# Carrying the recurrent state every 64 tokens instead of every 128, with 64x64 products four at a time, in batches 2 to 4 of an mLSTM and Fourier-mixing kernel

## The chip, the core and the metric

The kernel runs on one core of a Trainium2 chip. Its engines work side by side, each through its own queue in order: TensorE (PE in the profile: matmuls; PEld: its loads of stationary operands), VectorE (DVE), ScalarE (ACT), GpSimd (POOL) and SyncE (SP, which here issues the transfers). PSUM is the memory that TensorE writes; it has eight banks of 128 partitions x 512 fp32 numbers. The metric is the device time of one execution in microseconds; lower is better.

## The reference

There are two parts, one after the other. The first is an mLSTM cell for 4 batches, 8 heads, 768 tokens and head dimension 40. Per head it carries a 40x40 state `C`, a vector `n` and a stabilizing maximum `m`:

```python
m_new = np.maximum(f_gate[:, :, t] + m, i_gate[:, :, t])
f_stab = np.exp(f_gate[:, :, t] + m - m_new)
i_stab = np.exp(i_gate[:, :, t] - m_new)
C = f_stab * C + i_stab * outer(vt, kt)
n = f_stab * n + i_stab * kt
y[:, :, t] = sigmoid(o) * (C @ qt) / max(|n . qt|, 1)
```

The second part takes `y` as a (4, 768, 320) array `x`, and computes `u = x + real(fft over tokens and features of x)`, a normalization over the 320 features, and `u + relu(un @ w_ch1) @ w_ch2` with 1280 hidden features.

## The kernel before

**Tiling.** A batch's 768 tokens are 6 chunks of 128 (`L`, `NT`). Within a chunk the recurrence is a masked product, as in attention; between chunks a state of 41 columns per head (`C` and `n` together) is carried. Heads are held in pairs: the first head of a pair lies on partitions 0 to 39, the second on 64 to 103 (`hip` is 0 or 1). Per chunk of batches 2 to 4 (`b` is 1 to 3) the steps are:

- `mlstm_exp` (L421): 8 exponentials on ACT make the weights `W` of 128 x 128 per head. `mlstm_mask` (L443, POOL) zeroes what lies in the future.
- `mlstm_scores` (L465): 8 matmuls, keys by queries, 40 rows x 128 columns. `mlstm_weigh` (L471, DVE) multiplies them by `W`.
- `mlstm_scale_q` (L431) and `mlstm_scale_v` (L437), both POOL, make the decayed queries `qg` and the weighted values `vw`.
- `mlstm_from_state` (L479): 4 matmuls of 128 x 128 by 128, the state's share of the output, into a PSUM tile `ph`. `mlstm_from_chunk` (L486): 8 matmuls with 41 output columns add the chunk's own share.
- `mlstm_to_state` (L496): 8 matmuls make the state's new part `pc`; `mlstm_decay` (L455, POOL) and `mlstm_gather` (L513 or L515, DVE) update the state.
- `mlstm_gather` also copies `ph` to `hT` in SBUF (L517 to L528, ACT). `mlstm_turn` (L540) transposes `hT` by 4 matmuls with the identity, to `px`. `mlstm_finish` (L549 to L555) is five DVE operations that divide, apply the output gate and write the chunk's `x`.

The second part follows per batch: folding and Fourier products (`mix_...`), and the MLP (`mlp_...`: L861 for the first batch's first layer, L986 for its second; L923, L928 and L1042 for the later batches).

**Order.** Nothing is reordered after the program is written. A plan of slots fixes the order: `at(slot, phase, fn)` puts a step into a slot, and `run` issues the steps by slot and phase, on every engine in this order. Each slot has one step of some batch's MLP at phase `MAIN` (2); the chunks' work of a later batch is filled around it, at `FILL` (1) for other engines and `FILL_PE` (3) for TensorE. Chunk `c` of batch `b` begins at slot `s = s0 + 3c`, with `s0` 0, 32, 50, 82. From slot s + 3 on comes a block of TensorE work: from-state of chunk c, scores of chunk c + 1, from-chunk and to-state of chunk c. The turned output follows up to five slots later.

**PSUM.** Four banks belong to the MLP and the mixing (`bank`). Two are a ring for scores (`ps_s`), two a ring for `ph`, `pc` and `px` (`ps_h`): a new tile takes the bank whose last tile has been read. The program's accesses by two engines to one bank of a tile are put in program order with semaphores, reads after reads too.

## Time and profile before

| | |
|---|---|
| Time, median of 3 runs | 416.13 us (415.49 to 417.23) |
| The profiled execution's span, first to last instruction | 414.0 us |
| So what lies around the span, against the median | 2.1 us |
| TensorE busy | 404.0 us, 98% |
| VectorE busy | 289.3 us, 70% |
| ScalarE busy | 188.8 us, 46% |
| GpSimd busy | 115.7 us, 28% |

The profile names each group of instructions by line, engine, operation and tile. A matmul of fp32 data shows as two records, so 8 matmuls are x16. A timeline row gives the start in us from the span's start, the time from the first start to the last end, and what was run. As matmuls are pipelined, rows overlap: the time that TensorE gives to a group is the distance to the next group's start. In square brackets stands how long the engine was idle ahead of a row, and for whom.

### The profile page before, as it was taken

How to read it: one execution, taken by the hardware profiler on the slowest of the kernel's cores; microseconds unless marked ns; L12 is line 12 of the kernel's file. 1: busy time of each engine (PE TensorE's matmuls, PEld its weight loads, DVE VectorE, ACT ScalarE, POOL GpSimd, SP SyncE). 2: the span in 40 equal slices, each digit the busy share in tenths (PEclk: the TensorE clock that was granted, in tenths of full speed). 3: DMA queues.
4: the chain of work that ended last, by engine and by line, in shares of the span. 5: the costliest groups of instructions: out<-in, count | busy, mean ns of one | idle time of the engine just before them, and what ended most of it. 6: DMA issues, size and time to landing. Idle time of an engine off the chain costs nothing.

```text
span 414.0 us, 8020 instructions
## 1 busy us (share of the span) xinstructions
PE 404.0 (98%) x2966; PEld 304.2 (73%) x2966; DVE 289.3 (70%) x682; ACT 188.8 (46%) x493; POOL 115.7 (28%) x194
## 2 busy tenths in 40 slices
PE   8999999999999999999999999999999999999997
PEld 6877555666667778776559998976559988555996
DVE  8789894978885548777874569787863786335652
ACT  6986366686651232655455413745551113355000
POOL 5554201567442420342061430342040000020000
PEclk9999999999999999999999999999999999999999
DMA  7899298479564154266100544310000000000010
GB/s 227 291 251 334 71 275 265 132 223 289 187 193 148 61 153 143 63 213 205 45 0 2 156 152 132 95 50 1 0 2 0 33 32 34 0 0 2 22 43 32
DMA packets 20549, 47.14 MB, mean 114 GB/s; under 512 B 2784, under 2 KB 9312, under 8 KB 20384
## 3 DMA queue, kind: packets, MB, share of 16 engines
q1 hardware_dynamic: 20512, 46.65, 36.6%
q8 instruction: 23, 0.38, 0.4%
q14 instruction: 14, 0.11, 0.1%
HBM read 42.52 MB, written 4.11 MB: 113 GB/s over the span
## 4 chain that ended last, share of the span: by engine, by line
PE 88%; DVE 8%; ACT 2%; POOL 1%; issue 1%; ACTq 0%; DVEq 0%
PE po L1042 18%; PE pm L923 17%; PE po L986 8%; PE pm L928 6%; PE ph L486 5%; PE pm L861 5%; PE ps L465 5%; PE ph L479 4%; PE pu L740 3%; PE px L540 2%; PE pm L852 2%; PE pz L709 2%; PE put L783 2%; PE pc L496 1%; PE pz L697 1%; DVE stats L767 1%
## 5 line engine op out<-in xcount | busy, mean ns | idle before, releaser
L992 DVE SCALAR_TENSOR_TENSOR x<-po,rstd,x 128x160 f32<-128x160 f32 (+1 forms) x69 | 27.0, 394 | 41.1 <-PE po L1042 35.5
L932 DVE TENSOR_TENSOR h<-h,pm 128x384 f32<-128x384 f32 x60 | 30.6, 550 | 30.4 <-PE pm L928 17.4
L421 ACT ACTIVATE W<-W,colT 128x128 f32<-128x128 f32 x144 | 45.1, 395 | 0.0
L443 POOL TENSOR_SCALAR_AFFINE_SELECT W<-W 128x1024 f32<-128x1024 f32 x18 | 22.4, 1247 | 75.4 <-ACT W L421 54.5
L923 PE MATMUL pm<-uT,w_sb 128*128 128x384 f32 x90 | 37.5, 504 | 0.2 <-DVE uT L911 0.2
L986 PE MATMUL po<-w_sb,h 128*128 128x320 f32 x120 | 34.4, 435 | 0.0
L471 DVE TENSOR_TENSOR W<-ps,W 128x512 f32<-128x512 f32 x48 | 30.7, 681 | 2.6 <-POOL W L443 2.3
L861 PE MATMUL pm<-uT,w_sb 128*128 128x384 f32 x80 | 29.7, 498 | 0.1
L986 PEld LDWEIGHTS po<-w_sb,h 128*128 128x128 f32 x120 | 22.3, 190 | 9.4 <-issue 0.8
L1042 PE MATMUL po<-T,S 128*128 128x160 f32 x180 | 27.9, 302 | 0.3 <-DVE x L992 0.3
L788 ACT COPY uT<-put 128x384 f32<-128x384 f32 x24 | 11.2, 478 | 37.1 <-PE put L783 37.1
L465 PE MATMUL ps<-qk 40*128 40x128 f32 x384 | 27.4, 282 | 0.0
L465 PEld LDWEIGHTS ps<-qk 40*128 40x128 f32 x384 | 23.9, 188 | 4.6 <-issue 0.7
L1042 PEld LDWEIGHTS po<-T,S 128*128 128x128 f32 x180 | 25.5, 190 | 1.7 <-DVE x L992 0.5
L1042 PE MATMUL po<-w_sb,h 128*128 128x160 f32 x180 | 26.5, 302 | 0.0
L524 ACT COPY h<-ph 41x512 f32<-41x512 f32 (+1 forms) x16 | 9.3, 582 | 37.1 <-PE ph L486 37.0
L1042 PEld LDWEIGHTS po<-w_sb,h 128*128 128x128 f32 x180 | 25.2, 190 | 1.3 <-DVE x L992 0.3
L431 POOL TENSOR_TENSOR qg<-qk,Gb 128x512 f32<-128x512 f32 x18 | 26.1, 1449 | 0.1
L486 PE MATMUL ph<-W,kvt 128*41 128x128 f32 x384 | 25.8, 277 | 0.0
L923 PEld LDWEIGHTS pm<-uT,w_sb 128*128 128x128 f32 x90 | 15.4, 190 | 13.2 <-DVE h L932 6.0
L479 PEld LDWEIGHTS ph<-qg,C 128*128 128x128 f32 x160 | 20.2, 192 | 5.5 <-POOL qg L431 1.6
L979 ACT ACTIVATE h<-h 128x384 f32<-128x384 f32 x45 | 23.1, 521 | 2.0 <-DVE h L932 2.0
(207 smaller groups left out, 844.5 us busy)
## 6 DMA issues: line engine op xcount, KB each, us to landing
W<-M_d SPq DMA_DIRECT2D x18, 512.0 KB
kvt<-in_kv SPq DMA_DIRECT2D x24, 324.0 KB
qk<-in_qkT SPq DMA_DIRECT2D x48, 160.0 KB
raw<-in_w SPq DMA_DIRECT2D x10, 640.0 KB
Gb<-G_d SPq DMA_DIRECT2D x36, 128.0 KB
so<-in_o SPq DMA_DIRECT2D x24, 160.0 KB
out<-x SPq DMA_DIRECT2D x24, 160.0 KB
ds_sb<-in_dft_s SPq DMA_DIRECT2D x1, 1155.0 KB
```

The lines of the kernel that those rows point to most:

```text
L421: nc.scalar.activation(out=k.W[:, h, :], in_=M, func=AF.Exp, scale=-1.0, bias=colT[:, c, 0, b * H + h:b * H + h + 1])
L431: nc.gpsimd.tensor_tensor(out=k.qg, in0=k.qk[:, 0], in1=k.Gb, op=OP.mult)
L465: nc.tensor.matmul(k.ps[hip][:, p, :], k.qk[r, 1, p, :], k.qk[r, 0, p, :], start=True, stop=True)
L471: nc.vector.tensor_tensor(out=Wv, in0=k.ps[hip], in1=Wv, op=OP.mult)
L479: nc.tensor.matmul(k.ph[:, p, :], k.C[:, p, :], k.qg[:, p, :], start=(p == 0), stop=False, skip_group_check=True)
L486: nc.tensor.matmul(k.ph[hip * 64:hip * 64 + D1, p, :], k.v1[:, 2 * p + hip, :], k.W[:, 2 * p + hip, :], start=(c == 0 and p == 0), stop=Tr ...
L861: nc.tensor.matmul(k.pm[i], w1_sb[:, ch, f0:f0 + L], u[2 * ch], start=(ch == 0 and not ahead), stop=(ch == 1 and ahead), skip_group_check= ...
L923: nc.tensor.matmul(bank, w, u, start=start, stop=True, skip_group_check=True)
L932: nc.vector.tensor_tensor(out=h, in0=h, in1=bank, op=OP.add)
L986: nc.tensor.matmul(k.po, hidden(gr, f)[:, i * L:(i + 1) * L], w2_sb[:, f, :], start=(f == 0), stop=(f == NFF - 1))
L992: nc.vector.scalar_tensor_tensor(out=u, in0=po, scalar=k.rstd[:, c:c + 1], in1=u, op0=OP.mult, op1=OP.add)
L1042: nc.tensor.matmul(po, a[:, f], w[:, f], start=start and f == 0, stop=f == half - 1, skip_group_check=True)
```

## The change

In batches 2 to 4 the recurrence inside a chunk is done in two halves of 64 tokens (`LH`), and the state is carried from half to half. The first batch keeps its form.

- Each of the four products becomes 16 matmuls on 64x64 tiles: 64 or fewer rows, 64 columns, 64 (or 41) moving columns, in the order `TILES`, so that four in a row use the four quarters of the array. Scores and to-state stand together ahead of the second part of from-chunk; from-chunk is split in two (`turn` 0 and 1), as the quarters change banks, with a small ACT copy (`halves_between`) between.
- `W` holds 64 columns per head: half the bytes are loaded (two transfers), exponentiated and weighed; the mask takes two POOL operations.
- The state is updated twice per chunk (`halves_decay`, `halves_add`), once for each half, in full-width operations instead of one per `hip`.
- Two PSUM tiles of two banks each, `scores` and `heads`, take the place of the rings. Scores use the first half of each bank, `pc` the second half of the same; `ph` uses the first half of the two heads banks and `px`, the turned output, the second half. `halves_order` is a small ACT copy that reads both.
- The turned outputs come at slots s0 + 8, 11, 14, 17, 20, 20; `mlstm_finish` follows in the next slot (for the fifth chunk, in the same one).
- Decays and weights for halves are made once, in the first batch's slots 8 to 18 (`halves_of_chunks`).
- The layouts of `q`, `k`, `v` and the spread table change on the host to match.

```diff
--- before.py
+++ after.py
...
-    ps_s = pool("ps_s", 2, space=PSUM)
-    ps_h = pool("ps_h", 2, space=PSUM)
+    ps_s = pool("ps_s", 1, space=PSUM)
+    ps_h = pool("ps_h", 1, space=PSUM)
...
+    scores = ps_s.tile([L, 2, NP * L], FP, name="ps")
+    heads = ps_h.tile([L, 2, NP * L], FP, name="ph")
+    whole = {id(t): iter(range(10**6)) for t in (scores, heads)}
+    def whole_bank(t, *shape):
+        part = t[:, next(whole[id(t)]) % 2, 0:int(np.prod(shape))]
+        return part.rearrange("p (a b) -> p a b", b=shape[-1]) if len(shape) > 1 else part
...
+    states = [t.rearrange("p n t -> p (n t)")[:, i * 2 * L:(i + 1) * 2 * L] for t in C_bufs for i in range(2)]
...
+        def halves_of_chunks(step):
+            half, end = M[0:BH, :, LH:], M[0:BH, :, LH - 1:LH].to_broadcast([BH, NT, LH])
+            if step == 0:
+                late["G"], late["K"] = (gp.tile([BH, NT, LH], FP, name=n) for n in ("G2", "K2"))
+                nc.gpsimd.tensor_tensor(out=late["G"], in0=end, in1=half, op=OP.subtract)
+                nc.gpsimd.tensor_tensor(out=late["K"], in0=a[:, :, 0:LH], in1=end, op=OP.subtract)
+            elif step == 1:
+                nc.scalar.activation(out=g[0:BH, :, LH:], in_=late["G"], func=AF.Exp)
+                nc.scalar.activation(out=wk[:, :, 0:LH], in_=late["K"], func=AF.Exp)
+            elif step == 2:
+                d2 = late["dec2"] = w2_sb[0:BH, 0, 0:BH // 2 * NS].rearrange("p (n c) -> p n c", c=NS)
+                ends = g[0:BH].rearrange("p c (i t) -> p (c i) t", i=2)[:, :, LH - 1]
+                nc.gpsimd.tensor_tensor(out=d2, in0=ends.unsqueeze(1).to_broadcast([BH, BH // 2, NS]),
+                                        in1=spread_sb[:, L:].unsqueeze(2).to_broadcast([BH, BH // 2, NS]), op=OP.mult)
+            elif step == 3:
+                p2 = bank("p2", [L, NT * BH + BH // 2 * NS], 2)
+                pt, pd = p2[:, 0:NT * BH], p2[:, NT * BH:]
+                late["p2"] = [t.rearrange("p (n c) -> p n c", c=n) for t, n in ((pt, BH), (pd, NS))]
+                for c in range(NT):
+                    nc.tensor.transpose(late["p2"][0][:, c, :], wk[:, c, :], ident[0:BH, 0:BH])
+                nc.tensor.matmul(late["p2"][1], spread_sb[:, 0:L], late["dec2"], start=True, stop=True)
+            else:
+                pt, pd = late["p2"]
+                nc.vector.tensor_copy(out=colT[:, :, 1, H:], in_=pt[:, :, H:])
+                nc.vector.tensor_copy(out=decB[:, NP:], in_=pd[:, NP:])
...
+        for n, (s, phase) in enumerate(((8, FILL + 0.55), (10, FILL + 0.75), (12, FILL + 0.5), (17, FILL_PE + 0.5),
+                                        (18, FILL + 0.75))):
+            at(s, phase, halves_of_chunks, n)
...
     def mlstm_load_max(b, c):
         k = chunks[b, c]
-        k.W = wp.tile([L, H, L], FP, name="W", tag="W")
-        nc.sync.dma_start(out=k.W, in_=M_d[c, b * H:(b + 1) * H, :].unsqueeze(0).to_broadcast([L, H, L]))
+        k.W = wp.tile([L, H, L], FP, name="W", tag="W").rearrange("p h t -> p (h t)")[:, 0:H * LH]
+        k.W = k.W.rearrange("p (h t) -> p h t", t=LH)
+        for i in range(2):
+            nc.sync.dma_start(out=k.W[i * LH:(i + 1) * LH],
+                              in_=M_d[c, i, b * H:(b + 1) * H, :].unsqueeze(0).to_broadcast([LH, H, LH]))
...
     def mlstm_mask(b, c):
-        W = chunks[b, c].W
-        nc.gpsimd.affine_select(out=W, in_=W, compare_op=OP.is_ge, fill=0.0, base=0, pattern=[[0, H], [1, L]],
-                                channel_multiplier=-1)
+        for i in range(2):
+            W = chunks[b, c].W[i * LH:(i + 1) * LH]
+            nc.gpsimd.affine_select(out=W, in_=W, compare_op=OP.is_ge, fill=0.0, base=0, pattern=[[0, H], [1, LH]],
+                                    channel_multiplier=-1)
+    def product(out, w, x, start):
+        nc.tensor.matmul(out, w, x, start=start, stop=True, skip_group_check=True)
...
+    sides = heads.rearrange("p hip (s m t) -> p s hip m t", s=2, t=L)
+    TILES = ((0, 0), (1, 1), (0, 1), (1, 0))
+    def wide(t, n):
+        return t[:, n:n + LH]
+    def halves_scores(b, c):
+        k = chunks[b, c]
+        n = NP * LH
+        k.ps = scores[:, :, 0:n].rearrange("p hip (m t) -> p hip m t", t=LH)
+        k.pc = scores[:, :, n:n + NP * D1].rearrange("p i (m d) -> p i m d", d=D1)
+        for p in range(NP):
+            for hip, i in TILES:
+                r, t = slice(hip * 64, hip * 64 + D), slice(i * LH, (i + 1) * LH)
+                product(k.ps[t, hip, p, :], k.qk[r, 1, p, t], k.qk[r, 0, p, t], True)
+    def halves_to_state(b, c):
+        k = chunks[b, c]
+        for p in range(NP):
+            for i, hip in TILES:
+                if 2 * c + i < NS - 1:
+                    r, h = slice(i * LH, (i + 1) * LH), hip * NP + p
+                    product(k.pc[hip * 64:(hip + 1) * 64, i, p, :], wide(k.k[r], h * D), k.vw[r, h, :], True)
+    def halves_state(k, i):
+        return k.C[i][:, 0:NP * D1].rearrange("p (m d) -> p m d", d=D1)
+    def halves_decay(b, c, i):
+        k, n = chunks[b, c], 2 * c + i
+        if 0 < n < NS - 1:
+            nc.gpsimd.tensor_tensor(out=halves_state(k, i + 1), in0=halves_state(k, i),
+                                    in1=decB[:, b * NP:(b + 1) * NP, n].unsqueeze(2).to_broadcast([L, NP, D1]), op=OP.mult)
+    def halves_add(b, c, i):
+        k, n = chunks[b, c], 2 * c + i
+        if n == 0:
+            nc.vector.tensor_copy(out=halves_state(k, 1), in_=k.pc[:, 0])
+        elif n < NS - 1:
+            nc.vector.tensor_tensor(out=halves_state(k, i + 1), in0=halves_state(k, i + 1), in1=k.pc[:, i], op=OP.add)
+    def halves_weigh(b, c):
+        k = chunks[b, c]
+        W = k.W.rearrange("p (hip m) t -> p hip m t", hip=2)
+        nc.vector.tensor_tensor(out=W, in0=k.ps, in1=W, op=OP.mult)
+    def halves_from_state(b, c):
+        k = chunks[b, c]
+        k.ph = sides[:, 0]
+        for m in range(2):
+            for i in range(2):
+                for hip, side in TILES:
+                    if 2 * c + i > 0:
+                        r, t, p = slice(hip * 64, hip * 64 + D), slice(i * LH, (i + 1) * LH), 2 * m + side
+                        product(k.ph[side * 64:(side + 1) * 64, hip, m, t], wide(k.C[i][r], p * D1), k.qg[r, p, t],
+                                m == 0 and i == (c == 0))
+    def halves_from_chunk(b, c, turn):
+        k = chunks[b, c]
+        for m in range(2):
+            for i, side in TILES:
+                hip = i ^ turn
+                r, h = slice(i * LH, (i + 1) * LH), hip * NP + 2 * m + side
+                product(k.ph[side * 64:(side + 1) * 64, hip, m, r], wide(k.v[r], h * D1), k.W[r, h, :], False)
+    def halves_between(b, c):
+        nc.scalar.copy(out=warm[0:1, 0:1], in_=chunks[b, c].ph[0:1, 1, 1, L - 1:L])
+    def halves_order():
+        nc.scalar.copy(out=warm[0:1].rearrange("p (a b) -> p a b", b=2), in_=heads[0:1, :, 0:NP * L:2 * L])
+    def halves_gather(b, c):
+        k = chunks[b, c]
+        k.hT = hT_bufs[(b * NT + c) % 2]
+        mlstm_heads(b, c, k.ph)
+    def halves_turn(b, c):
+        k = chunks[b, c]
+        px = sides[:, 0 if c == NT - 2 else 1]
+        for p in range(NP):
+            nc.tensor.transpose(px[:, p // 2, p % 2], k.hT[:, p, :], ident)
+        k.px = px
...
-        h1 = k.px.rearrange("p pr (two e) -> p (pr two) e", two=2)
+        px = k.px.rearrange("p (a pr) t -> p a pr t", a=2) if b == 0 else k.px
+        h1 = px.rearrange("p a pr (two e) -> p a (pr two) e", two=2)
...
+    def plan_halves(b, s0, stride=3):
+        for c in range(NT):
+            s = s0 + stride * c
+            end = c == NT - 1
+            t = 22 + 2 * c if b == 1 and c < 3 else s - 5
+            at(t, FILL, mlstm_load, b, c)
+            at(t, FILL, mlstm_load_max, b, c)
+            at(t, FILL, mlstm_load_decay, b, c)
+            at(s, FILL, mlstm_load_o, b, c)
+            at(s - 1, FILL, mlstm_scale_v, b, c)
+            at(s, FILL, mlstm_exp, b, c, 0)
+            at(s, FILL_PE + 2.05, halves_scores, b, c)
+            at(s, FILL_PE + 2.5, halves_to_state, b, c)
+            for i in range(2):
+                at(s + i, FILL + 0.05, halves_decay, b, c, i)
+                at(s + 1 + i, FILL - 0.2, halves_add, b, c, i)
+            at(s + 1, FILL - 0.5, mlstm_exp, b, c, NP)
+            at(s + 1, FILL, mlstm_mask, b, c)
+            at(s + 1, FILL + 0.1, mlstm_scale_q, b, c)
+            at(s + 2, FILL, halves_weigh, b, c)
+            at(s + 3, MAIN - 0.1 if end else FILL_PE, halves_from_state, b, c)
+            at(s + 3, MAIN - 0.1 if end else FILL_PE, halves_from_chunk, b, c, 0)
+            at(s + 3, MAIN if end else FILL_PE + 0.5, halves_between, b, c)
+            at(s + 3, FILL_PE + 3, halves_from_chunk, b, c, 1)
+            at(s + 4, FILL, halves_gather, b, c)
+            at(s + 4, FILL + 0.35, mlstm_tanh, b, c)
+            t = s0 + (8, 11, 14, 17, 20, 20)[c]
+            if c < NT - 2:
+                at(t - 1, FILL + 0.3, halves_order)
+            at(t, FILL_PE + 0.5 if c < NT - 2 else MAIN - 0.1, halves_turn, b, c)
+            if c < NT - 1:
+                at(t + 1, FILL + 0.05, halves_order)
+            first = c == NT - 2
+            at(t + (not first), MAIN + 0.55 if first else FILL + 0.05, mlstm_finish, b, c)
...
-        plan_mlstm(b, s_mlstm)
-        done = [s_mlstm + 3 * (j + NT // 2) + 7 + (b > 0 and j == 0) for j in range(NT // 2)]
+        (plan_halves if b > 0 else plan_mlstm)(b, s_mlstm)
+        done = [s_mlstm + n for n in ((16, 19, 22) if b == 0 else (18, 21, 22))]
```

## The prediction

> **What bounds the kernel now.** I read first the page's busy shares, then TensorE's groups by shape, then the timeline around a chunk's block, and last TensorE's waits.
>
> ```profile
> PE 404.0 (98%) x2966; PEld 304.2 (73%) x2966; DVE 289.3 (70%) x682; ACT 188.8 (46%) x493; POOL 115.7 (28%) x194
> ...
> PE   8999999999999999999999999999999999999997
> ...
> DVE  8789894978885548777874569787863786335652
> ```
>
> TensorE is the bound in every slice; DVE is near it in many (8 and 9 tenths). So TensorE time taken out counts in full, until a wait takes its place.
>
> ```profile
> L465 PE MATMUL ps<-qk 40*128 40x128 f32 x384 | 27.4, 282 | 0.0
> ...
> L486 PE MATMUL ph<-W,kvt 128*41 128x128 f32 x384 | 25.8, 277 | 0.0
> ...
> L479 PE MATMUL ph<-qg,C 128*128 128x128 f32 x160 | 21.5, 278 | 2.0 <-POOL qg L431 1.0 <-ACT C L511 0.8 <-DVE x L555 0.2
> ...
> L496 PE MATMUL pc<-vw,kvt 128*40 128x41 f32 x320 | 9.5, 202 | 0.0
> ```
>
> These are the four products. The next view is the timeline of the third batch-2 block (ordered by start):
>
> ```profile
> 105.29 1.29 DVE L471 TENSOR_TENSOR W<-ps,W 128x512 f32<-128x512 f32 x2
> ...
> 106.49 0.15 DVE L549 TENSOR_SCALAR den<-px 128x8 f32<-128x8 f32 x1
> ...
> 106.99 2.44 ACT L421 ACTIVATE W<-W,colT 128x128 f32<-128x128 f32 x8
> ...
> 107.65 0.49 DVE L555 TENSOR_TENSOR x<-px,so 128x320 f32<-128x320 f32 x1
> ...
> 108.21 1.05 PE L479 MATMUL ph<-qg,C 128*128 128x128 f32 x8
> ...
> 109.19 1.16 PE L465 MATMUL ps<-qk 40*128 40x128 f32 x16
> ...
> 110.28 1.07 PE L486 MATMUL ph<-W,kvt 128*41 128x128 f32 x16
> ...
> 111.19 0.48 PE L496 MATMUL pc<-vw,kvt 128*40 128x41 f32 x16
> ...
> 111.59 0.91 PE L861 MATMUL pm<-uT,w_sb 128*128 128x384 f32 x2
> ```
>
> The block takes 111.59 - 108.21 = 3.38 us. A turn's 4 records take 0.44 us (112.34 to 112.78), so a record of 128 columns takes 110 ns. From-state is 8 of these, 0.88; the other products' 16 records run two at a time: 0.88, 0.88, and 8 x 110 x 41/128 = 0.28 for to-state. What is left, 0.46, is the cost of changing the tile shape, 0.1 to 0.2 each time. `mlstm_finish` takes 1.65 us (106.49 to 108.14) and here ends 0.07 us ahead of from-state. Earlier in this batch:
>
> ```profile
> 96.99 0.60 PE L540 MATMUL px<-ident,h 128*128 128x128 f32 x4
> ...
> 97.63 0.17 DVE L549 TENSOR_SCALAR den<-px 128x8 f32<-128x8 f32 x1 [0.35 <-PE px L540]
> ...
> 98.08 1.05 PE L479 MATMUL ph<-qg,C 128*128 128x128 f32 x8
> ...
> 98.82 0.49 DVE L555 TENSOR_TENSOR x<-px,so 128x320 f32<-128x320 f32 x1
> ```
>
> Here from-state starts 1.23 us ahead of the end of finish: today the two use different banks.
>
> **What the Trainium skill says.** "TensorEngine Tiling (Array Packing)", Tiling Modes: 64x64 gives four independent tiles, and a change of mode drains the array; the 0.1 to 0.2 us agree with the second, no run here shows four tiles. "TensorE: Matmul & The Clock Gate", Wait — 56ns, not 53.3ns?: starts never come closer than about 25 ns. The trace differs: to-state's 16 records, each 202 ns, fit into 0.48, so their starts are (480 - 202)/15 = 19 ns apart. "PSUM — Partial Sum Buffer", PSUM bank collisions raise a hardware error: two engines mustn't touch one bank and quadrant at once, even at other columns. So a turned output that DVE still reads blocks TensorE's next write into that bank.
>
> **The change, part by part.**
>
> *Products.* Each of the four becomes 16 matmuls, 32 records of 64 columns, in 8 rounds of four. A round takes 110/2 = 55, say 57 ns; to-state too, as its loads are now 64 wide. Bounds: 57 ns if four overlap, 105 if only two do or starts keep 25 ns apart. I take 57, since pairs overlap fully in both directions today. Rounds per batch: scores 48, from-chunk 48, from-state 44, to-state 44: 184 x 0.057 = 10.5 us, against 5 x 0.88 + 12 x 0.88 + 5 x 0.28 = 16.4. Shape changes: two per block (0.35) and one extra pair at the last, 2.8 against 3.0. Per batch 6.1, in all **-18.3 us**.
>
> *Preparation.* 6 transposes (12 records; L249's 12 take 1.5 us busy with drains, some 0.06 each) and a matmul of 192 columns, 0.33: **+1.1** in batch 1, with its POOL, ACT and DVE work beside MLP and mixing (if not covered, another 1).
>
> *DVE, ACT, POOL, DMA.* Weighing is one operation of 0.68 instead of two; exponentials fall from 0.31 to an estimated 0.25 each; mask and decays take about the same; loads of `W` halve, at one more issue on SP per chunk. All of it lies under TensorE's MLP steps: nothing. Were that cover gone, DVE's 0.68 per chunk would be worth up to 12 us.
>
> *Turned outputs in the heads banks.* From-state of slots s0 + 9, 12, 15, 18 now waits until `mlstm_finish` of the same slot has read `px`. The chain from a turn's end: 0.05, `halves_order` 0.17 (an ACT copy of 4 columns takes that), 0.05, finish 1.65, 0.15 to the first product: 2.1 us, seen from TensorE's free moment 2.2, less the MLP step in between. Behind exponentials in ACT's queue the copy comes 1.0 later, behind a ReLU pair too (0.85) 1.9 later. Behind the waiting from-state stand, on TensorE, the rest of the block and the next MLP step; behind the waiting finish, on DVE, the additions of that slot's MLP step, for which TensorE waits only later.
>
> - Batch 2: steps of 1.94, 0.65, 1.94 and 0 us lie between, the last since from-state of the last chunk stands ahead of `MAIN`, right after the turn. Waits 2.0, 1.6, 1.4, 2.2.
> - Batch 3: at the first place finish ended at 161.70 in the trace, behind the mixing's additions, from-state began at 159.28; less 0.6 for the weighing, 1.8. Then 0.2, 0.2 (steps of 2.7 and 3.0 us cover), 2.2.
> - Batch 4: 0.5, 1.8 (step of 1.36, ACT's exponentials start only at 266.68), 0.2, 2.2.
>
> In all **+16.3**. Bounds: 6.6 (only the three places without a step between) and 26 (2.2 at each).
>
> *Other waits.* The second part of from-chunk waits for `halves_between`: 0.16 + 0.05 + 0.17 + 0.15 = 0.5 us, under 16 rounds of scores and to-state (0.9): nothing, if ACT is free; it holds back the next four exponentials behind it, which have 3 us to spare. The first `qg` of batch 2 was late already (1.0 us before 78.11); a decay now stands ahead of it on POOL and TensorE comes earlier: **+1.0**. Slack lost at other places, bounds 0 and 5: **+1.5**. To-state moves three slots earlier, and with it the weighting of values on POOL (0.77) one slot, behind the previous chunk's mask and `qg`; POOL is 28% busy: nothing, and 0.8 at each of 18 blocks at worst. The loads stay in their slots. The fold of pair (1, 4) moves two slots later, 2.1 us of DVE under two 2.7 us steps: nothing.
>
> Sum on the span: 414.0 - 18.3 + 1.1 + 16.3 + 1.0 + 1.5 = 415.6; with the 2.1 us around it 417.7.
>
> **Rivals.**
>
> *Four tiles run, waits small (faster).* For it: from-state has slack where MLP steps are 2.7 us; only the three bare places remain. 414.0 - 18.3 + 1.1 + 6.6 + 1.0 + 2.1 = 406.5. Against it: at 98.08 today from-state doesn't wait, and couldn't otherwise start.
>
> *DVE takes finish late (slower).* At 96.99 finish followed its turn at once, but in batch 3 it began 4.4 us after it (160.08 against 155.66), in batch 4 as late (255.17 against 250.76). If the twelve waits average 2.2 us, they cost 26: 427. It decides from a mean of 1.7 on.
>
> *Four tiles don't overlap (slower).* Rounds of 105 ns: + 552 x 0.048 = 26.5, of which a third is given back by shorter waits: 435. For it: nothing here has run four. Against it: pairs of rows and pairs of columns both do. This is the case in which the change doesn't do what it says.
>
> **How the numbers follow.** Waits eat the gain, 412 to 422: 0.45, likeliest, 417.7. Small waits, 401 to 411: 0.25. Late finish, 422 to 431: 0.18. No overlap, 431 to 441: 0.12. The range 404 to 431 leaves out some 0.07 below and 0.12 above. About 0.5% (2.1 us) is what a measurement of this kernel can tell from none. Faster: 0.24 of the second case and 0.05 of the first, 0.29; same, 414.05 to 418.2: 0.23; slower: 0.18 of the first and the last two, 0.48.
>
> **What would show it.** Right: the groups of 64x64 products busy about half as long as today; from-state's waits named as finish's last DVE operation, some 12 of them, 16 us in all, three of 2.2 us right after a turn; TensorE's share under 95%. Wrong: from-state's waits under 8 us in all; rounds near 105 ns; or a long wait elsewhere, such as the second part of from-chunk for `halves_between`, or the first products of batch 2.

## The result, and the profile after

The change makes the kernel slower. It took 431.94 us (median of 4 runs, 430.80 to 435.13) against 416.51 us (4 runs, 415.49 to 417.23): a ratio of 1.038, 95% interval 1.034 to 1.043. The prediction was 417.7, its range 404 to 431. The profiled execution of the changed kernel is the longest of the four: span 433.4 us, 1.7 us around it; the one before had 414.0. In the ratios here and below, a run more than 1.5% above the fastest of its kernel is left out; medians and ranges hold every run unless the text says otherwise.

The page of the changed kernel, its busy time and two rows of its 40 slices; line numbers from here on are those of the changed kernel:

```profile
PE 400.9 (93%) x4246; PEld 292.4 (67%) x4246; DVE 276.3 (64%) x669; ACT 183.6 (42%) x537; POOL 123.9 (29%) x227
...
PE   8987799798879999897999999987999999999997
...
PEclk9999899698998999999899999999999999999999
```

TensorE was busy 98% of a shorter span; now it is 93%, so 22.5 us of idle time are new (28.2 against 5.7, counted from TensorE's first matmul to its last). And the last line has digits that were all 9 before: in some slices TensorE was granted a lower clock.

The four products, one group for each (the helper `product` is L498):

```profile
L498 PE MATMUL ph<-W,kvt 64*64 64x64 f32 x576 | 17.7, 236 | 3.8 <-DVE W L646 3.4 <-ACT warm L673 0.4
L498 PE MATMUL ps<-qk 40*64 40x64 f32 x576 | 12.6, 225 | 0.0
L498 PE MATMUL ps<-vw,kvt 64*64 64x41 f32 x528 | 12.4, 232 | 0.0
L498 PE MATMUL ph<-qg,C 40*64 40x64 f32 x528 | 12.2, 230 | 15.1 <-DVE x L710 15.0
```

Busy time fell from 84.2 us (with batch 1; three quarters of it are 63) to 54.9, which holds stretches at a lower clock too. It fell as was wanted, and a round of four takes the time that was forecast: at full clock the 8 rounds of scores stand 0.47 us before the next product, 58 ns each, and a block takes 2.03 us instead of 3.38. In the last of these lines stands the wait that was forecast, 15.0 us of from-state for the last operation of `mlstm_finish`. One of its places, in the timeline (start, length, what was run, and in brackets the idle time ahead of it):

```profile
127.34 0.66 PE L688 MATMUL ph<-ident,h 128*128 128x128 f32 x4
128.08 0.15 ACT L677 COPY warm<-ph 1x4 f32<-1x4 f32 x1 [0.80 <-PE ph L688]
128.27 0.17 DVE L703 TENSOR_SCALAR den<-ph 128x8 f32<-128x8 f32 x1 [1.56 <-ACT warm L677]
...
129.46 0.49 DVE L710 TENSOR_TENSOR x<-ph,so 128x320 f32<-128x320 f32 x1
...
130.09 0.69 PE L498 MATMUL ph<-qg,C 40*64 40x64 f32 x32 [2.10 <-DVE x L710]
```

This is the chain of the prediction, turn, order copy, finish, from-state, with its 2.1 us. What had not been forecast comes behind it. The next view gives busy time and granted clock (PEclk) of four stretches of 3.41 us, two pairs that follow each other:

```profile
core 0: us, PE busy (x) PEld busy (x) DVE busy (x) ACT busy (x) POOL busy (x), PEclk, DMA share, GB/s
...
100.15:103.57 3.42, 1.29 (x82) 1.25 (x85) 2.89 (x7) 0.55 (x5) 0.84 (x3) 1.00 0.57 152
103.57:106.98 3.41, 3.41 (x65) 2.21 (x57) 2.44 (x6) 1.98 (x8) 2.26 (x4) 0.50 0.98 313
...
171.83:175.25 3.42, 1.85 (x7) 0.95 (x5) 3.21 (x12) 0.00 (x0) 0.00 (x0) 1.00 0.49 151
175.25:178.66 3.41, 3.17 (x134) 2.95 (x135) 1.29 (x6) 0.71 (x3) 0.00 (x0) 1.00 0.49 149
```

Behind the wait of 2.12 us at 100.23, TensorE runs the whole next stretch at half clock; behind the wait of 1.81 at 173.68 it doesn't. There are six such places in the trace (48.95, 79.67, 103.57, 130.87, 205.97, 301.54), one of them twice as long, 23.9 us in all; TensorE was busy in 22.8 of them. In them a record of 384 columns starts 0.64 to 0.80 us ahead of the next one, elsewhere 0.32. At half the speed, 11.4 us of TensorE's time were lost (an estimate, half of 22.8). All stretches lie on one grid of 3.413 us. The four runs had mean clocks of 0.972, 0.980, 0.988 and 0.992 and took 435.1, 433.0, 430.9 and 430.8 us. These clocks stand for some seven, five, three and two stretches at half clock: how many waits fall so that they fill a stretch of the grid differs from run to run. Between the first and the last of these runs, five stretches fewer came with 4.3 us less, some 0.9 for each and not 1.7: part of what the clock costs seems to come back, as waits get shorter when TensorE is slower (not shown).

The longest waits of TensorE are these (total, times, longest):

```profile
PE ph L498 <- DVE x L710: 15.0, 10, 2.1
PE ph L498 <- DVE W L646: 3.4, 2, 3.1
PE ph L596 <- DVE x L710: 2.5, 1, 2.5
PE ph L532 <- POOL fe L797: 1.5, 1, 1.5
```

The second row is for the most part at the first block of batch 2, where I had priced a wait for `qg` at 1.0 more. In the timeline there, and in SP's queue:

```profile
72.28 1.08 SPq L458 DMA_DIRECT2D Gb<-G_d  x2
73.46 0.54 SPq L376 DMA_DIRECT2D raw<-in_w  x1
...
79.01 0.49 DVE L386 TENSOR_SCALAR e<-raw 128x640 uint32<-128x640 uint32 x1 [9.81 <-DMA raw<-in_w]
...
80.06 0.68 DVE L646 TENSOR_TENSOR W<-ps,W 128x512 f32<-128x512 f32 x1
...
80.80 0.71 PE L498 MATMUL ph<-W,kvt 64*64 64x64 f32 x16 [3.05 <-DVE W L646]
```

SP had issued nothing from 64.2 to 72.3: it waited for a buffer of the third chunk's decays. The change gives the first chunk of each later batch decays too (its second half needs them), so two buffers are one too few here until POOL has used the first. Behind that load stand two weight slabs; DVE waits 9.8 us for one, and the weighing stands behind it.

The last two rows of the waits are in the first batch:

```profile
46.11 0.17 DVE L703 TENSOR_SCALAR den<-ph 128x8 f32<-128x8 f32 x1 [3.58 <-ACT h L575]
...
47.89 0.66 PE L596 MATMUL ph<-ident,h 128*128 128x128 f32 x4 [2.50 <-DVE x L710]
```

The finish of chunk 5 waits for the gather of chunk 6, and the last turn for that finish, though they use different banks: the two banks are now one tile (`heads`), and the program orders their users. The first mixing product starts 5.0 us later, before and after:

```profile
43.38 0.49 PE L706 MATMUL pz<-ds_sb,fe 128*128 128x193 f32 x2
...
48.38 0.49 PE L879 MATMUL pz<-ds_sb,fe 128*128 128x193 f32 x2
```

### The profile page after: what moved, and what is told of

Its sections match the earlier page's. It is cut to its first block, busy times and chain, and to the rows that moved or that the text cites. A ratio compares the mean times of both kernels' runs of the same rounds, so it can differ in the third digit from the quotient of the medians.

```text
span 433.4 us, 10669 instructions
## 1 busy us (share of the span) xinstructions
PE 400.9 (93%) x4246; PEld 292.4 (67%) x4246; DVE 276.3 (64%) x669; ACT 183.6 (42%) x537; POOL 123.9 (29%) x227
## 4 chain that ended last, share of the span: by engine, by line
PE 67%; DVE 17%; issue 7%; ACT 3%; DMA 3%; POOL 1%; SPq 1%; ACTq 0%; POOLq 0%; DVEq 0%
PE po L1215 17%; PE pm L1096 14%; PE po L1159 6%; PE pm L1101 5%; PE ph L498 5%; PE ps L498 3%; DVE so L707 2%; PE pm L1034 2%; PE pu L913 2%; DVE x L710 2%; DMA kvt<-in_kv 1%; PE ph L688 1%; DMA raw<-in_w 1%; PE pz L870 1%; PE put L956 1%
## 5 line engine op out<-in xcount | busy, mean ns | idle before, releaser
L494 POOL TENSOR_SCALAR_AFFINE_SELECT W<-W 64x512 f32<-64x512 f32 x36 | 25.1, 696 | 100.1 <-ACT W L471 98.9
L471 ACT ACTIVATE W<-W,colT 128x64 f32<-128x64 f32 x144 | 38.1, 338 | 0.0
L1096 PE MATMUL pm<-uT,w_sb 128*128 128x384 f32 x90 | 37.8, 512 | 0.2 <-DVE uT L1084 0.2
L1034 PE MATMUL pm<-uT,w_sb 128*128 128x384 f32 x80 | 31.4, 527 | 0.1
L1101 PE MATMUL pm<-uT,w1t_sb 64*128 64x384 f32 x120 | 25.9, 510 | 0.7 <-DVE h L1105 0.7
L498 PE MATMUL ph<-qg,C 40*64 40x64 f32 x528 | 12.2, 230 | 15.1 <-DVE x L710 15.0
L481 POOL TENSOR_TENSOR qg<-qk,Gb 128x512 f32<-128x512 f32 (+1 forms) x21 | 26.0, 1239 | 0.3
L673 ACT COPY warm<-ph 1x1 f32<-1x1 f32 x18 | 2.6, 147 | 54.9 <-PE ph L498 54.9
L1096 PEld LDWEIGHTS pm<-uT,w_sb 128*128 128x128 f32 x90 | 16.3, 195 | 14.0 <-DVE h L1105 3.6
L498 PEld LDWEIGHTS ph<-qg,C 40*64 40x64 f32 x528 | 10.1, 139 | 22.0 <-issue 17.1
L980 POOL TENSOR_TENSOR t<-rstd 128x6 f32<-128x6 f32 x12 | 3.1, 257 | 64.8 <-DVE v L974 64.3
L1101 PEld LDWEIGHTS pm<-uT,w1t_sb 64*128 64x128 f32 x120 | 12.9, 185 | 12.7 <-issue 8.2
```

What stands on the lines that cost most here:

```text
L471: nc.scalar.activation(out=k.W[:, h, :], in_=M, func=AF.Exp, scale=-1.0, bias=colT[:, c, 0, b * H + h:b * H + h + 1])
L481: nc.gpsimd.tensor_tensor(out=k.qg[:, :, t], in0=k.qk[:, 0, :, t], in1=k.Gb[:, :, t], op=OP.mult)
L494: nc.gpsimd.affine_select(out=W, in_=W, compare_op=OP.is_ge, fill=0.0, base=0, pattern=[[0, H], [1, LH]], channel_multiplier=-1)
L498: nc.tensor.matmul(out, w, x, start=start, stop=True, skip_group_check=True)
L1034: nc.tensor.matmul(k.pm[i], w1_sb[:, ch, f0:f0 + L], u[2 * ch], start=(ch == 0 and not ahead), stop=(ch == 1 and ahead), skip_group_check= ...
L1096: nc.tensor.matmul(bank, w, u, start=start, stop=True, skip_group_check=True)
```

## The experiments

My theory after the trace: the loss is idle time of TensorE from three sources (finish, SP's queue, the first batch's one tile), and the clock that falls behind long idle time. Rivals: the waits move elsewhere when one is taken out; the clock falls because of the 64x64 products. All kernels below compute the full result. Ratios are to the kernel before, times in us; each edit is shown against the changed kernel unless the text says otherwise, with `...` where lines are left out.

| edit | median | ratio, 95% interval |
|---|---|---|
| the change | 431.94 | 1.038 (1.034 to 1.043) |
| sixth from-state behind the MLP step | 427.73 | 1.027 (1.022 to 1.033) |
| turns ahead of the MLP step | 426.79 | 1.027 (1.024 to 1.029) |
| one Gb load later in SP's queue | 427.02 | 1.029 (1.023 to 1.035) |
| first batch's output in its own bank | 431.49 | 1.037 (1.034 to 1.039) |
| products of zeros in four waits | 439.17 | 1.053 (1.047 to 1.060) |
| the four edits together | 413.78 | 0.994 (0.992 to 0.996) |
| ... without the first batch's | 416.68 | 1.000 (0.998 to 1.002) |
| ... with the slabs first in SP's queue | 412.11 | 0.989 (0.987 to 0.992) |
| ... and two small moves | 411.70 | 0.989 (0.988 to 0.990) |

### Waits for finish

```diff
-            at(s + 3, MAIN - 0.1 if end else FILL_PE, halves_from_state, b, c)
-            at(s + 3, MAIN - 0.1 if end else FILL_PE, halves_from_chunk, b, c, 0)
-            at(s + 3, MAIN if end else FILL_PE + 0.5, halves_between, b, c)
+            at(s + 3, FILL_PE, halves_from_state, b, c)
+            at(s + 3, FILL_PE, halves_from_chunk, b, c, 0)
+            at(s + 3, FILL_PE + 0.5, halves_between, b, c)
```

> The sixth chunk's from-state and the first half of its from-chunk go behind the MLP step of their slot instead of ahead of it (batches 2 to 4), so that a step of 2 to 3 us lies between the turn of chunk 4 and the from-state that waits for its finish. Theory 'waits, and the clock behind them': the three waits of 2.1 us (at 127.99, 203.90 and 298.11 of the changed kernel's trace) fall to 0.2 each or less, the half-clock stretches behind them (130.87, 205.97, 301.54) go, and the time falls by 6 for the waits and 3 to 5 for the clock, to 421 to 424. Rival 'the wait only moves': finish or ACT's copy is late anyway, TensorE waits as long one step on; 430 to 432. Rival 'the 64x64 products pull the clock down, not the waits': the waits go, the half-clock stretches stay; 425 to 426.

The profiled one of its four executions took 1359.5 us, so its trace says nothing of the waits; the other three took 428.2, 429.9 and 434.5. The same kernel once more:

> The same kernel as the first of these experiments (the sixth chunk's from-state behind its slot's MLP step), run again, as its profiled execution was disturbed and shows nothing. Undisturbed times so far: 428.2 to 434.5. Theory 'waits, and the clock behind them': in the profile the three waits of 2.1 us are gone, and no half-clock stretch lies within 5 us behind these three places; time 427 to 430. Rival 'the wait only moves': a wait of 1.5 us or more one MLP step on, at each of the three places.

It took 427.73 (425.69 to 430.25). The three waits of 2.1 us became 0.6, 0.8 and 0.8, and no half-clock stretch lies behind the second and third. Behind the first place lies one, but there TensorE stood still for 3.0 us with no cause named (128.76 to 131.73); more on that below. At the other two places no long wait comes back one step later (0.3 us for the copy between the halves). The gain, 4.2, is short of the first expectation; over the seven usable executions of both series the median is 428.2, a gain of 3.7.

```diff
-            at(t, FILL_PE + 0.5 if c < NT - 2 else MAIN - 0.1, halves_turn, b, c)
-            if c < NT - 1:
-                at(t + 1, FILL + 0.05, halves_order)
-            first = c == NT - 2
+            at(t, MAIN - 0.1, halves_turn, b, c)
+            first = c < NT - 1
+            if first:
+                at(*((t, MAIN + 0.5) if c < NT - 2 else (t + 1, FILL + 0.05)), halves_order)
```

> The turns of chunks 1 to 4 of batches 2 to 4 go ahead of the MLP step of their slot instead of behind it, and their order copy and finish follow in the same slot: one more MLP step (0.65 to 3 us) between each turn and the from-state that waits. Theory 'waits, and the clock behind them': of the 14.6 us of from-state's waits for finish 2 to 4 are left, the four half-clock stretches behind them go; 432 less 11 and less 3 to 6: 415 to 418. Rival 'the wait moves to the turn': the turn itself now waits for the gather of the next chunk and for the order copy in ACT's queue, 0.5 to 1 us at each of nine places; 422 to 426. Rival 'DVE is the limit': finish starts no earlier, since DVE's queue is full with the MLP's additions; 428 to 432.

426.79 (425.05 to 428.12), a gain of 5.2 where 14 to 17 were expected. Finish waits fell from 15.0 to 6.0, as expected; but 2.2 and two of 1.7 are left. The 2.2 (at 108.42) and the last 1.7 (at 288.38) have half clock behind them, as have the first batch's and the weighing's waits: 17.1 us at half clock in its profile. The 1.7 at 198.59, which is split over two stretches of the grid, has not. One wait of 0.9 moved to a turn, so the first rival holds in a small part. That 9.0 us less of finish waits gave only 5.2 isn't explained by this.

### SP's queue

```diff
-            at(t, FILL, mlstm_load_decay, b, c)
+            at(*((s0 + 1, FILL + 0.65) if (b, c) == (1, 2) else (t, FILL)), mlstm_load_decay, b, c)
```

> One load is moved in SP's queue: the decays (Gb) of batch 2's third chunk are loaded in slot 33, behind the scaled queries of the first chunk that free their buffer, instead of in slot 26. Theory 'SP stood still': in the changed kernel SP waits from 64.2 to 72.3 us for that buffer, the two weight slabs behind it come late, DVE waits 9.8 us for one of them and weighs the first chunk late, and TensorE waits 3.05 us for that (77.74) and falls to half clock for 6.8 us (79.67 to 86.50). All three go: the wait falls to 1 us or less, the time by 2 to 5.5, to 427 to 430. Rival 'the slabs are late because the DMA engines are full': slab and wait stay where they are, 431 to 433.

427.02 (426.55 to 432.12), the upper end of the expected gain: moving one load is worth 4.9. In its timeline:

```profile
70.58 0.72 DVE L386 TENSOR_SCALAR e<-raw 128x640 uint32<-128x640 uint32 x1 [2.68 <-DMA raw<-in_w]
...
76.26 0.41 PE L498 MATMUL ph<-W,kvt 64*64 64x64 f32 x16
```

The slab is there 8.4 us earlier and from-chunk doesn't wait at all. A wait of 1.73 comes instead at the next block (84.06), where DVE joins that slab ahead of the weighing. The slabs were late by SP's order, not by the DMA engines.

### The first batch

```diff
...
-        k.px = bank("px", [L, NP, L]) if early else whole_bank(heads, NP, L)
+        k.px = bank("px", [L, NP, L], 1 if c == NT - 2 else None) if early else whole_bank(heads, NP, L)
...
-            at(t, FILL_PE + (2.5 if c < 4 else 1), mlstm_turn, b, c, c < 4)
+            at(t, FILL_PE + (2.5 if c < 4 else 1), mlstm_turn, b, c, c < NT - 1)
```

> In the first batch the fifth chunk's turned output goes into a bank of its own (one of the MLP's, free at that place), and the sixth chunk's product tile takes the other half of the two heads banks. Theory 'one tile for both banks': in the changed kernel the finish of chunk 5 waits 3.6 us for the gather of chunk 6, and the last turn 2.5 us for that finish; a wait of 1.45 us comes ahead of chunk 6's from-state. With separate banks these come down to 0.8 each as before the change, the first mixing product starts at 44 to 45.5 us instead of 48.4, the half-clock stretch at 48.95 goes; the time falls by 3 to 5, to 427 to 429. Rival 'the preparation of halves costs it': six transposes, a product and two copies, 0.9 us of TensorE, stay; the first mixing product at 47.5 or later, 430 to 432.

431.49 (430.53 to 432.49): no gain that can be told from none, a miss; time and first mixing product lie where the rival, the preparation, had put them. Yet the last turn's wait fell from 2.50 to 0.81 and the half-clock stretch at 48.95 went. The wait of 1.46 stayed at 1.46, and the first mixing product still starts at 47.58. This trace is 0.9 us later already at the scores of chunk 6 (36.12 against 35.24); counted from there the mixing product comes 1.7 us earlier, which is what the wait lost. The turn of chunk 4 and what follows are late already at 38.1, for DVE. My reading was that what was won was swallowed by the next wait, the weighing's, which SP's queue timed. The two traces don't bear that out: TensorE is 2.4 us earlier ahead of that wait (MLP's first products at 61.64 against 64.04) and 3.3 us earlier behind it (77.51 against 80.80), and the profiled execution took 3.8 us less than that of the change. What hides the gain in the medians may be the clock: all four runs stand at 0.980 to 0.984, but two of the change's four at 0.988 and 0.992. The kernel with the other edits but without this one:

> The four edits together less the one on the first batch: its fifth output is again in the heads tile. On its own that edit brought 0.5 us, though it took a wait of 2.5 us to 0.8; behind it in the unchanged schedule stood a wait of TensorE for DVE that SP's queue timed, not TensorE. Theory 'the gain was swallowed by the next wait': without that next wait (the Gb load is moved here) the edit is worth its wait and the half-clock stretch behind it: this kernel takes 2 to 4 us more than the four together, 415.5 to 418. Rival 'the wait in the first batch never cost anything': 413 to 414.5, as the four together.

416.68 against 413.78 with it: with the other three edits in place, the edit is worth 2.9 us. The theory's number holds, and its rival, that the wait never cost anything, is out; its account of the swallowed gain is not what the traces show.

### The clock

```diff
...
+            if (b, c) in ((1, 2), (1, 5), (2, 5), (3, 5)):
+                at(s + 3, (MAIN - 0.1 if end else FILL_PE) - 0.05, keep_busy, 8)
             at(s + 3, MAIN - 0.1 if end else FILL_PE, halves_from_state, b, c)
```

> Nothing is taken away from the waits; into the four longest of them (from-state of the third and sixth chunk of batch 2, of the sixth of batches 3 and 4) go eight products of zeros each, 128 x 92, some 1.2 us, into columns of the scores banks that nothing uses. Theory 'idle TensorE lowers its clock': with 0.9 us idle in place of 2.1 no half-clock stretch follows these four places, and those behind other waits stay; the from-state begins when it did, and the time falls by what the clock took there, 1.7 us for each stretch, of which some half came back from shorter waits later: 427 to 430. Rival 'the clock falls for another reason' (the 64x64 products, a limit by time): the stretches stay, 431 to 433. Rival 'the products of zeros push the rest': each place 0.3 us later at worst, 433.

439.17 (435.01 to 441.46): slower than expected by any theory. In its profile (435.0 us) the waits at the four filled places are 0.3 us or less, and no stretch at half clock follows any of them directly (the one at 127.58 stands behind a stop of 1.5 us in the block that follows the second): on the clock the first theory holds. But the four groups took 1.9 us each, not 1.2, and TensorE stands still at two new places, 2.0 and 1.5 us, with no cause named. Why its other runs took 3.9 to 6.5 us more than the profiled one isn't settled. As a price of the clock this run is inconclusive.

The kernels with few waits give an estimate of the price, since the same program ran with different clocks. That with the slabs first (below) took 410.3, 410.9 and 411.1 at a mean clock of 0.999 to 1.0, and 413.1, 413.3 and 413.5 at 0.996; one stretch of 3.41 us at half clock in 411 us gives 0.996. So a run with one stretch takes 2.5 us more there. The four edits together, in 19 of their 20 runs (all but the longest), took 410.5 at 1.0, a mean of 413.3 at 0.995 to 0.996, 414.4 at 0.992 and 416.3 at 0.988, some 2 us for each stretch, but with up to 3.8 us between runs of one clock. In the changed kernel it was 0.9. Half the clock for 3.41 us is 1.7 us of TensorE's work; what goes beyond it may be the longer wait that lowered the clock in these runs. The times don't part the two.

### All together

> All four edits together: the turns and the sixth from-state moved by an MLP step each, the Gb load moved in SP's queue, the first batch's fifth output in a bank of its own. Theory 'three kinds of wait and the clock behind them': TensorE's idle time falls from 28 us to 9 to 12, half-clock stretches are gone or one, and the time is the kernel before less 16 for the products, plus 0.9 for the preparation and 4 to 7 of idle time more than before: 404 to 412. If the gains overlap (a wait removed at one place lets DVE be late at the next): 412 to 418. Rival 'DVE is the limit now': TensorE waits for DVE's weighing and additions instead, 418 to 424.

413.78 (410.52 to 417.37): the middle case, gains that overlap. Idle time in its profile is 15.4 us, where 9 to 12 were expected. It beats the kernel before by 0.6%, as it should if the products' gain was there and waits and clock ate it. The edits were not tried on the kernel before; what they could gain there is bounded by its 5.7 us of idle time. One wait of 2.3 us was left because slabs in SP's queue still stood behind other Gb loads (against the four edits):

```diff
-            at(*((s0 + 1, FILL + 0.65) if (b, c) == (1, 2) else (t, FILL)), mlstm_load_decay, b, c)
+            after_slab = {2: s0 + 1, 3: t + 1, 4: t + 1, 5: t + 1} if b == 1 else {}
+            at(*((after_slab[c], FILL + 0.75) if c in after_slab else (t, FILL)), mlstm_load_decay, b, c)
```

> The four edits together, and in batch 2 the Gb loads of chunks 3 to 6 go behind the weight slabs in SP's queue (in the four together only that of chunk 3 was moved, and to a place ahead of the slab). In that kernel's trace the slabs still stand behind Gb loads that wait for POOL (at 84.70, 96.36 and 103.45), DVE waits 3.3 us for a slab at 103.78 with the finish of chunk 1 behind it, and TensorE 2.3 us for that (105.64). Theory 'SP's order makes DVE late': both go, the waits of batch 2 fall by 2 to 4 us, and the stretch of half clock behind with them: 408 to 412. Rival 'the slabs are late by their own buffer' (a slab's buffer comes free only when DVE has joined the one before): nothing changes, 413 to 414.5.

412.11 (410.34 to 413.54), just past the upper end of the expectation. The 2.3 us wait became 0.75, and its profile, the fastest of the six runs, shows no half clock while TensorE works:

```profile
PEclk9999999999999999999999999999999999999999
```

This is 1.1% faster than the kernel before. One wait of 1.73 was left; taking it away (against the kernel just above):

```diff
-        if c == NT - 1:
+        if c >= NT - 2:
             next(whole[id(heads)])
...
-            at(s + 2, FILL, halves_weigh, b, c)
+            at(*((s + 1, FILL + 0.65) if (b, c) == (1, 1) else (s + 2, FILL)), halves_weigh, b, c)
```

> The kernel before this (four edits, and the slabs ahead in SP's queue) with two small moves: chunk 2 of batch 2 is weighed one step earlier on DVE, ahead of the taking of a weight slab, and the first batch's last two product tiles change banks. That kernel had one wait of 1.73 us left (82.35, for that weighing), and its runs fell into two groups, 410.3 to 411.1 at full clock and 413.1 to 413.5 with one half-clock stretch. Theory 'a wait close to the limit of the clock': with the wait at 0.2 us no run has a stretch; all times lie within 1 us, at 408.5 to 410. Rival 'the stretch comes from elsewhere' (the first batch, the 64x64 blocks): two groups again, 409 to 410 and 411.5 to 412.5.

411.70. Six of its eight runs were at full clock and took 411.1 to 412.4; one with one stretch at half clock took 413.0, and the longest, with about four, 417.4. So the stretches did not go from all runs, as the theory had it, and two of eight against three of six before are too few to say that the wait near the limit set the clock. 408.5 to 410 was a miss too: at full clock the kernel is 0.8 us slower than the one above (means of 411.6 and 410.8). The wait for the weighing gave way to one of 1.2 for the copy between the halves, and TensorE stood still for 1.6 us without a named cause (120.35). The bank swap left the wait in the first batch at 1.46, and why isn't settled.

### The unnamed stops, and the price of a round

In several kernels above TensorE stops inside or right behind blocks of 64x64 products, for 1.5 to 3.0 us, and waits for nothing that the profile shows. TensorE's instructions come in transfers of 16 KB. With 128 more instructions at the start (32 products of one column), the place of such a transfer moves:

> The four edits together, and 32 products of one column of zeros more at the very start, where TensorE waits for the gates: 128 instructions more on TensorE and otherwise the same program. In the four together TensorE stands still for 1.8 us in the middle of a block of 64x64 products (126.19 to 128.00), with nothing named that it waits for; an instruction fetch starts 0.6 us before it, and TensorE goes on 2.45 us after that start. Theory 'the block runs ahead of the instruction fetch': the still stretch leaves this place, and none or another is found, again with a fetch that starts within 1 us of it. Rival 'something in this block makes TensorE wait' (a bank, a change of tile shape): it stays at the same instruction. Time 412 to 416 in either case.

The stop at 126 is gone and there is no other. The time, 427.94, is my error: the 32 products held TensorE until 18.23 us instead of 4.35. Less these 13.9, it is 414.0, within the expectation. But these 13.9 us also move the block against everything else, so this run alone doesn't tell a shifted transfer from a shifted time. The next edit (against the last kernel above, with the two small moves) prices a round and makes the blocks denser:

```diff
-        for p in range(NP):
+        for p in [p for p in range(NP) for _ in range(2)]:
             for hip, i in TILES:
                 r, t = slice(hip * 64, hip * 64 + D), slice(i * LH, (i + 1) * LH)
                 product(k.ps[t, hip, p, :], k.qk[r, 1, p, t], k.qk[r, 0, p, t], True)
```

> The kernel just above with every 64x64 score product of batches 2 to 4 issued twice (the second overwrites the first with the same numbers), to price a round of four by itself: 18 chunks x 4 rounds of two records = 144 rounds more. Theory 'four tiles run at once': 57 to 59 ns a round, 8.2 to 8.5 us more than the kernel above. Rival 'four tiles overlap only partly': 105 ns a round, 15 us more. Rival 'the instruction stream is the limit of dense 64x64 work': still stretches of TensorE with no named cause appear in the blocks, and the time grows by 12 us or more though the rounds in the trace stay at 57 to 59 ns.

It took 425.9 and 426.9; two more runs, with more stretches at half clock, 433.6 and 434.6. In the traces the scores take 8.38 us more of TensorE, 58.2 ns for each of the 144 rounds: four tiles do run at once. The rest of the 14 us is the third case. TensorE's waits in this kernel, and the longest stop in the timeline:

```profile
PE ph L498 <- issue: 5.6, 2, 4.3
...
PE ps L498 <- issue: 1.4, 1, 1.4
```

```profile
104.95 0.25 PE L498 MATMUL ph<-W,kvt 64*64 64x64 f32 x1
109.46 0.70 PE L498 MATMUL ph<-W,kvt 64*64 64x64 f32 x15 [4.26 <-issue]
```

"issue" is idle time for which the profile shows no cause. Three stops, 7.0 us in all, where the kernel with single scores had one of 1.6. In the traces of five kernels there are eight such stops of over 1 us behind 60 us; in each of them a 16 KB instruction transfer starts between 1.1 us ahead of the stop and 1.6 into it, and TensorE goes on 2.4 to 2.6 us after that start. A block is 256 instructions in 2.0 us (128 matmuls and their weight loads), and 16 KB hold as many by the counts (33 transfers for 8,575 recorded instructions). The stops stand at the borders of such portions. With the shorter ones, down to 0.07 us, there are twelve, and TensorE had started 2497, 2753, 3009, 3777 or 7361 of its recorded instructions when it stopped, each time 193 more than a multiple of 256. So TensorE stands still until the next 256 instructions can be used, in these twelve 2.4 to 2.7 us after their transfer starts. What decides when their transfer starts is open: the kernel with the slabs first has the same instructions on TensorE as the four edits together, and no stop over 0.4 us. The stop of 1.8 us in the four edits and the 1.6 in the last kernel above stand at the same border, 3009; the transfer for it had started at 2961 and 2944 instructions there, and at 2760 with the slabs first.

## Why the prediction was wrong, point by point

The sum was 415.6 on the span; the profiled execution took 433.4, 17.8 more.

**Products, -18.3: right.** The four products of batches 2 to 4 take 56.2 us of TensorE before and 36.9 at full clock (in the kernel with the slabs first): -19.3. The rival of rounds of 105 ns, whose 435 is nearest to the result, is refuted: 58 ns.

**Waits of from-state, +16.3: right.** 15.0 us, named as forecast, with three of 2.1 right behind a turn (2.10, 2.08, 2.08). The places: 2.1, 1.4, 0.5, 2.1 in batch 2; 1.8, 0, 0.3, 2.1 in batch 3; 0.9, 1.6, 0.1, 2.1 in batch 4. The mean of the twelve is 1.25 us, below the 1.7 from which the rival of a late finish decides. The third place of batch 2 was off by 0.9 us, the others by 0.4 or less.

**Preparation, +1.1 in batch 1: right in itself (0.9 us of TensorE at 42.84), but the step was too small.** It looked at what `halves_of_chunks` adds and not at what the first batch loses when two rings of banks become one tile. The first mixing product came 5.0 us late.

**The first `qg` at +1.0, and DVE, ACT, POOL and DMA at nothing because "The loads stay in their slots": wrong.** The loads stay in their slots, but there is one more of decays per batch, in a pool of two buffers, and SP's queue stood still for 8 us behind it. The prediction counted SP's extra issues and not the buffer that SP waits for. One moved load gave back 4.9 us. A long wait at the first products of batch 2 stood among the prediction's signs of being wrong, and it came: 3.05 us.

The `qg` wait of 1.0 and the slack of 1.5 were 2.5 us of idle time in the forecast; 22.5 - 15.0 = 7.5 came, with what the first batch lost.

**Not in the sum at all: the clock.** A wait was priced at its length. In this trace long waits at six places also brought half the clock for the next stretch of 3.41 us (at one place for two), 11.4 us of TensorE's time. This is the step that failed by most: a wait's price was its length, and what follows it was put at nothing. Without it the profiled span would be 422 by this sum, and 427 if a stretch costs the 0.9 us that the four runs suggest (433.4 less seven times 0.9); either is inside the range. The waits were called by their right size, and slower had the largest single chance (0.48); what was not asked is what a long idle time does to TensorE afterwards.

**MLP products in pairs.** At 196.8, 218.8 and 313.0 us of the changed kernel's trace, groups of the MLP's products with 64 rows take 2.1 to 2.4 us, idle time not counted, instead of 1.4 to 1.6 for the same groups before. Two products that otherwise run at once then run one after the other. In two of the three the wait for DVE stands in the middle of the group:

```profile
PE pm L1101 <- DVE h L1105: 0.7, 2, 0.4
```

That is 2.3 us in all that no idle time shows. The corrections add up to: products -1.0, finish waits -1.3, preparation -0.2, other idle time +5.0, clock +11.4, pairs +2.3: 16.2 of the 17.8. The rest isn't attributed.

## What to carry to other kernels

Price a wait of TensorE not by its length alone: here one that left more than 2.0 us of a 3.41 us stretch idle always had half clock behind it, which by the runs' times goes with 0.9 to 2.5 us more. Moving one step of other work into such waits shortened them, and the half clock behind went at two places out of three (first experiment). When a change adds one more user to a pool of buffers or joins two buffers to one tile, look for who stands behind the waiting load or reader in its queue, in the stages that the change was not meant to touch. With these waits shortened by edits, the kernel with the change is 1.1% faster than the one before.

## What the runs showed of the hardware that I had not expected

- **The clock falls sooner than by a whole idle stretch.** The Trainium skill, "TensorE: Matmul & The Clock Gate", HAM oscillation, says that "no PE-idle gaps >~3.4µs" is the abstract rule; its Part 1 has the free-running stretch of 3413 ns, which the grid here agrees with. In the thirteen usable profiles, before included, all 19 stretches at full clock with more than 2.0 us idle were followed by one at half clock; of the 18 between 1.5 and 2.0, 7 were (among them 1.53, 1.59, 1.72) and 11 not (1.58, 1.81, 1.96); of 1,477 under 1.5, one was (1.20). A stretch already at half clock was followed by another with as little as 0.23 us idle, but not every time (0.36).
- **Starts 14 to 15 ns apart on average.** Records of four 64x64 tiles start 14 to 15 ns apart on average (0.47 us for 32): in a block of the kernel with the slabs first, 5 to 11 ns apart within a round of four, and 35 or 36 ns ahead of the next round. The prediction's average of 19 ns for two tiles was no floor.
- **Dense small products can outrun their instructions.** Stops of 1.4 to 4.3 us with no cause named, eight of eight with a 16 KB instruction transfer started 2.4 to 2.6 us ahead of their end, and all at a border between portions of 256 instructions.
